# A list schedule with the measured hold of SBUF, K in one piece, and one square sum for V

## The chip, the cores and the metric

The kernel runs on one core of a Trainium2 chip. The core has five instruction queues that matter here: PE (TensorE, matmuls and their weight loads), DVE (VectorE), ACT (ScalarE), POOL (GpSimd) and SP, which here only issues DMAs. Each queue runs its instructions strictly in the order in which they stand; an instruction that waits holds all that stand behind it. The metric is the device time of one execution in microseconds (us); the time before is the median of three runs.

## The reference

```python
def _attn_ref(q, k, v):                         # B=8, H=8, S=1152, D=64
    q_pool = q.reshape(B, H, S // 2, 2, D).mean(axis=3)
    scores = 1 / np.sqrt(D) * np.matmul(q_pool, k.transpose(0, 1, 3, 2))
    attn = softmax(scores)                      # over the keys, row maximum subtracted
    return np.matmul(attn, v)

def _moe_ref(x, w_in, w_spatial, b_spatial, w_out):   # x: 8 x 576 x 512
    h = np.maximum(x @ w_in, 0.0)               # 512 x 1024
    u, v = h[..., :512], h[..., 512:]
    v_n = (v - v.mean(-1)) / np.sqrt(v.var(-1) + 1e-06)
    v_s = np.einsum('ts,bsd->btd', w_spatial, v_n) + b_spatial[None, :, None]
    return (u * v_s) @ w_out
```

All inputs are fp32 (two weight matrices are fp64 in DRAM). The kernel keeps nearly fp32 accuracy with fp16 matmuls: each factor is scaled by a power of two and split into a head (its fp16 value) and a rest (what the head leaves), and the products head x head, head x rest and rest x head are summed.

## The kernel before, in words

**Attention.** The 64 heads are taken as 32 pairs, `i = 0 .. 31`. For a pair, `prep(i)` makes the split factors: squares of K and of the pooled Q are summed on ACT (L569, L571, through `square_sum`, L381), a small matmul with ones (L360) and a few DVE operations (L365 to L371) turn the sums into scales, ACT writes the heads (`head`, L384), and the rests are written by DVE (`rest`, L387: `src * scale - head`, two inputs in SBUF) in the first eight pairs (`i < EARLY`), and by POOL in the others (L605, after ACT has scaled K in place, L602, and copied it to fp16, L604). K is worked on in two pieces of 640 and 512 columns. DMAs on SP (L591 to L614) then copy heads and rests to the partitions where the matmuls want them. `maxima(i)` runs 27 matmuls of 128x384 (L641, and L632 for the middle tile) and after each a DVE reduction (L647); `shift` (L660 to L670) makes of the row maxima a small tile that is transposed on PE (L668) and copied back. Two PSUM buffers (`pm`) serve the maxima, so PE waits for DVE when the reductions fall two behind. `attention(i)` runs the score matmuls (L842, L843) into three PSUM buffers (`pss`), ACT takes exp (L848), POOL splits the fp32 result into a bf16 top and an fp16 rest (L868; two inputs in SBUF), and `values` runs three groups of four small matmuls (L745, L751, L756), the last of which needs POOL's result.

**V.** `norm_v(i)` sums the squares of V, one head at a time (L519), `split_v(i)` writes its head and rest (L543 to L550).

**The gated unit.** After every eight pairs a `gated_unit` of two batches is interleaved with the following pairs: matmuls L926, L990, L1031 and L1074, and on DVE the `normalise` steps (L962 to L974) and at its gate the rests of the gated product (`rest`, L387, tile `vv`). All of these DVE steps read SBUF with two inputs, or in a copying form. There are four units; units 0 to 2 run beside attention, the last alone. In the first eight pairs the weights are loaded and converted from fp64 beside attention, by DVE steps of 128x1024 (L399 to L411).

**What sets the order.** The code is recorded in a rough order, and then `Order.pin` (L187) reorders it: it is a list scheduler that plays the program on the five queues with a cost for each instruction (`cost`, L148) and pins the order that results. Once pinned, nothing of the plan's times is left, only the order on each queue. Of an instruction on lane `m` that needs the result of lane `e`, the planner thinks it due at the result's planned end, plus a delay (`DELAY`), plus a reserve (`SLACK`, L38). For the time in which POOL and DVE hold each other off at SBUF it keeps two marks: `held` is the interval of POOL's last operation, `dve` the end of DVE's last operation of that kind. The operations concerned are those for which `two_from_sbuf` (L182) is true (`shared`). A DVE operation that would start after POOL's planned start is put off to 130 ns before POOL's planned end (L227 to L230, L239 to L247).

Of the kernel before, what the change touches and what calls it, by code (L numbers as in the profile page):

```python
# [10 lines left out]
F16 = mybir.dt.float16  # L11
BF16 = mybir.dt.bfloat16
F32 = mybir.dt.float32
# [18 lines left out]
class Order:  # L32

    LANES = ("PE", "Activation", "DVE", "Pool", "SP")
    DELAY = {("PE", "Activation"): 114, ("Activation", "Pool"): 77}
    SLACK = {("Pool", "PE"): 2100, ("Activation", "PE"): 300, ("DVE", "PE"): 300, ("SP", "PE"): 500}  # L38
    SIZE = {F16: 2, BF16: 2, F32: 4, I32: 4, U32: 4, I64: 8}

    def __init__(self):
# [106 lines left out]
    def cost(self, lane, ins):  # L148

        xs = [x.bass_ap for x in list(ins.ins) + list(ins.outs) if hasattr(x, "bass_ap")]  # L150
        count = lambda ap: math.prod([d[1] for d in ap.ap][1:])
        if lane == "PE":
            n = count(xs[0])
            t = max(28.5, n / 2.4 + 2.5)
            if xs[0].dtype == F32:
                t = 110 if n == 128 else max(224, 4 * n / 2.4)
            return t, t + 148
        if lane == "SP":
            big = max((count(x) * x.ap[0][1] * self.SIZE[x.dtype] for x in xs), default=0)
            return (1230 if "Transpose" in ins.opcode else 560), 2400 + big / (100 if "Transpose" in ins.opcode else 230)  # L160
        n = max((count(x) for x in xs), default=1)
        psum = any(self.slot.get(x.tensor.name, (0, 0))[1] for x in xs)

        flat = sum(count(x) == 1 for x in xs[:-1]) if n > 1 else 0
        wide = len(xs) - 1 - flat
        if lane == "Activation":
            t = 0.84 * n + (157 if psum else 188) + 85 * (min(flat, 2) or (n == 1 and wide > 1))
            if len(ins.outs) > 1:
                return t - 10, t + 95
            return t - 105, t  # L170
        elif lane == "DVE":
            plain = ins.opcode == "TensorScalarPtr"
            if plain and wide < 2 and not psum or ins.opcode == "TensorCopy":
                t = 0.55 * n + 140 + 60 * flat
            else:
                t = 1.04 * n + 145 + 65 * (flat > 0 and plain)
        else:
            t = {F32: 2.1, F16: 2.0, BF16: 1.74}[xs[1].dtype] * n + 150
            return t - 42, t
        return t - 84, t  # L180

# [5 lines left out]
    def pin(self, tc):  # L187
        names = {getattr(mybir.EngineType, e): e for e in self.LANES}
        fixed = ("RegisterMove", "TensorScalarAffineSelect", "Memset")
        prog = [i for i in tc.nc.cur_bb.bb.instructions if i.engine in names and i.opcode not in fixed]  # L190
        before, begun = self.edges(prog)
        loose = {i.name for a, z, skip in self.lined if skip for i in tc.nc.cur_bb.bb.instructions[a:z]}
        early = {i.name for i in tc.nc.cur_bb.bb.instructions[: self.seen]} - loose
        ahead = None
        for n, i in enumerate(prog):
            if names[i.engine] == "SP" and i.name not in loose:
                if ahead is not None and ahead not in before[n]:
                    begun[n].add(ahead)
                if i.name in early:
                    ahead = n  # L200
        after = [[] for _ in prog]
        left = []
        lane = [names[i.engine] for i in prog]
        for n, (pre, beg) in enumerate(zip(before, begun)):
            left.append(len(pre) + len(beg))
            for m in pre:
                after[m].append((n, True))
            for m in beg:
                after[m].append((n, False))
        cost = [self.cost(e, i) for e, i in zip(lane, prog)]  # L210
        shared = [e in ("DVE", "Pool") and self.two_from_sbuf(i) for e, i in zip(lane, prog)]
        held, dve = (0.0, 0.0), 0.0
        ready = {e: [n for n in range(len(prog)) if lane[n] == e and not left[n]] for e in self.LANES}
        due = [0.0] * len(prog)
        there = [0.0] * len(prog)
        free = dict.fromkeys(self.LANES, 0.0)
        wire = 0.0
        load = {n for n, i in enumerate(prog) if lane[n] == "SP" and i.ins and i.ins[0].bass_ap.tensor.name not in self.slot}
        last = {}
        dep = mybir.DependencyInfo(mybir.DependencyClass.NoSync, mybir.DependencyReason.DATA)  # L220
        for _ in prog:
            best = None
            for e, ns in ready.items():
                if ns:

                    at = {n: max(due[n], wire - 1000) if n in load else due[n] for n in ns}
                    if e == "DVE":  # L227
                        for n in ns:
                            if shared[n] and max(free[e], at[n]) >= held[0]:
                                at[n] = max(at[n], held[1] - 130)  # L230
                    t = max(free[e], min(at.values()))
                    n = min(n for n in ns if at[n] <= t)
                    if best is None or t < best[0]:
                        best = (t, e, n)
            t, e, n = best
            ready[e].remove(n)
            own, out = cost[n]
            t = max(free[e], there[n])
            if shared[n]:  # L239

                if e == "DVE":
                    if t >= held[0]:
                        t = max(t, held[1] - 130)
                    dve = t + out
                else:
                    t = max(t, dve)
                    held = (t, t + out)  # L247
            if e == "SP":
                wire = max(wire, t + own) + (out - 2400)
                end = wire + 1700  # L250
            else:
                end = t + out
            free[e] = t + own
            if e in last:
                tc.add_manual_dep(prog[n], last[e], dep, reason="order")
            last[e] = prog[n].name
            for m, through in after[n]:
                left[m] -= 1
                if not through:
                    x = t  # L260
                elif lane[m] != e:
                    x = end + self.DELAY.get((e, lane[m]), 52)
                else:
                    x = t if e == "PE" else end + 34
                there[m] = max(there[m], x)
                due[m] = max(due[m], x + (self.SLACK.get((e, lane[m]), 0) if through else 0))
                if not left[m]:
                    ready[lane[m]].append(m)
        self.span = max(free.values())
# [3 lines left out]
def attn_sgu_kernel(ctx: ExitStack, tc: tile.TileContext, qT, kT, v, w_in, w_spT, b_sp, w_out, out):  # L273
    nc = tc.nc
    P = 128
    B, NHP, _, D, _, S = qT.shape
    NC = kT.shape[4]
# [29 lines left out]
    sm = order.pool(ctx.enter_context(tc.tile_pool(name="sm", bufs=1)), 1)  # L307
# [43 lines left out]
    ws_l = const.tile([P, 5, S], F16, name="ws_l")  # L351
# [28 lines left out]
    def square_sum(acc, src, junk):  # L380
        nc.scalar.activation(junk, src, AF.Square, bias=0.0, scale=1.0, accum_out=acc)  # L381
# [127 lines left out]
    def norm_v(i):  # L509

        b, hp = divmod(i, NHP)
        if hp == 0:
            vsq[b] = sm.tile([P, 2 * NHP], F32, name="vsq", bufs=2)
        vt = load_v(i)
        yield
        yield
        for h in range(2):
            junk = vt[:, h] if b else ws_l[:, 0].rearrange("p (c d) -> p c d", d=D)
            square_sum(vsq[b][:, 2 * hp + h : 2 * hp + h + 1], vt[:, h], junk)  # L519
            yield  # L520
        if hp == NHP - 1:
            vscale[b] = yield from scale_of(vsq.pop(b), "v")
            yield
# [35 lines left out]
    def prep(i):  # L559
# [33 lines left out]
        for h, (a, rows) in enumerate(((MAIN, lower), (0, upper))):  # L593
            nc.sync.dma_start(out=qd[i % 2][rows, h], in_=X[rows, 0, a : a + TAIL])
        kn = st["kn"] = ld.tile([P, NC, P], F16, name="kn")
        for a, z in ((0, 5), (5, NC)):
            if i < EARLY:
                head(kn[:, a:z], k0[:, a:z], s_k)
                yield
                rest(KL[:, 0, a:z], k0[:, a:z], s_k, kn[:, a:z])  # L600
            else:
                nc.scalar.activation(k0[:, a:z], k0[:, a:z], AF.Copy, bias=0.0, scale=s_k)  # L602
                yield
                nc.scalar.activation(kn[:, a:z], k0[:, a:z], AF.Copy, bias=0.0, scale=1.0)  # L604
                nc.gpsimd.tensor_sub(KL[:, 0, a:z], k0[:, a:z], kn[:, a:z])  # L605
            yield
# [627 lines left out]
```

## Time and profile before

| | |
|---|---|
| median of three runs | 1219.08 us (1217.67 to 1220.74) |
| the profiled execution: its own time | 1220.91 us |
| the profiled execution: span of its instructions | 1219.1 us |
| PE busy | 1160.2 us, 95% |
| DVE busy | 887.9 us, 73% |
| ACT busy | 890.8 us, 73% |
| POOL busy | 841.1 us, 69% |
| DMA | 132.97 MB, mean 109 GB/s |

Busy is time in which an engine has an instruction under way. Matmuls overlap in PE's pipeline, and an operation that stands still because another engine holds what it needs counts as busy too; so "busy" is not "at its peak". In the rows, L12 is line 12 of the kernel, `mt<-pm` reads "writes tile mt, reads tile pm", and what stands in square brackets in a timeline is the idle time ahead of an instruction and who ended it.

### The profile page before, as it was taken

The page shows a single profiled execution, that of the slowest core. Times are in us where ns is not written, and L with a number is a line of the kernel's source. Part 1 is how long each engine was busy: PE and PEld are TensorE (multiplying, and loading weights), DVE is VectorE, ACT ScalarE, POOL GpSimd, SP SyncE. Part 2 cuts the span into 40 slices and gives each one's busy share as a digit, 9 for nine tenths or more (in the row PEclk, how much of TensorE's full clock was granted, in tenths as well). Part 3 has the DMA queues.
Part 4 walks back from the last instruction along what each step waited for, and adds up shares of the span by engine and source line. Part 5 has one row for each costly group of instructions (what it writes and reads, how often), then busy time and mean ns, then how long its engine had stood idle before and what let it go on. Part 6 is the DMA issues. An engine that isn't in the chain of part 4 may idle for free.

```text
span 1219.1 us, 33464 instructions
## 1 busy us (share of the span) xinstructions
PE 1160.2 (95%) x13296; PEld 726.5 (60%) x13296; DVE 887.9 (73%) x2228; ACT 890.8 (73%) x1675; POOL 841.1 (69%) x726
## 2 busy tenths in 40 slices
PE   3988999999998999999999999999999999999998
PEld 1656666766655666566665666566665666655453
DVE  5699989987889577766679676865669866841644
ACT  4887779789976877978777877878776876744433
POOL 2545657678886878888887887788887786874000
PEclk9889999999999999999999999999999999999999
DMA  5455455445432454255442443256334421211002
GB/s 190 163 156 161 123 178 143 125 119 153 130 87 77 138 123 123 73 158 152 114 101 75 125 140 82 65 143 204 99 98 103 103 70 49 48 47 45 1 1 79
DMA packets 88446, 132.97 MB, mean 109 GB/s; under 512 B 39840, under 2 KB 48032, under 8 KB 87776
## 3 DMA queue, kind: packets, MB, share of 16 engines
q1 hardware_dynamic: 88288, 130.82, 38.4%
q8 instruction: 104, 1.70, 0.6%
q14 instruction: 54, 0.44, 0.1%
HBM read 81.20 MB, written 9.44 MB: 74 GB/s over the span
## 4 chain that ended last, share of the span: by engine, by line
PE 71%; DVE 22%; issue 2%; ACT 1%; DMA 1%; POOL 0%; SPq 0%; DVEq 0%; ACTq 0%
DVE mt L647 8%; PE pss L842 7%; PE pss L843 7%; PE pm L641 7%; PE pw L1031 7%; PE pw L926 6%; PE pw L1074 5%; PE pw L990 5%; PE o L745 4%; PE o L756 4%; PE o L751 4%; DVE vv L387 2%; PE o L738 1%; DVE row L962 1%; PE pss L926 1%
## 5 line engine op out<-in xcount | busy, mean ns | idle before, releaser
L868 POOL TENSOR_TENSOR pt<-pt 128x512 f16<-128x512 f32 x528 | 574.1, 1103 | 195.8 <-ACT pt L848 193.0
L848 ACT ACTIVATE pt<-pss,esc 128x512 f32<-128x512 f32 x576 | 388.3, 689 | 140.4 <-PE pss L843 124.7
L647 DVE TENSOR_REDUCE mt<-pm 128x1 f32<-128x384 f32 x733 | 387.9, 551 | 102.3 <-PE pm L641 84.0
L842 PE MATMUL pss<-qhi,khi 128*128 128x512 f16 x576 | 220.9, 384 | 2.0 <-ACT pt L848 1.7
L843 PE MATMUL pss<-xq,klo 66*128 66x512 f16 x576 | 221.6, 386 | 0.0
L641 PE MATMUL pm<-khi,qhi 128*128 128x384 f16 x655 | 204.0, 329 | 17.7 <-DVE mt L647 12.6
L745 PEld LDWEIGHTS <-pt 128*128 128x128 bf16 x2112 | 119.3, 99 | 62.2 <-DVE xm L764 6.5
L745 PE MATMUL o<-vp,pt 128*128 128x65 f16 x2112 | 155.1, 193 | 0.7 <-DVE xm L764 0.4
L756 PE MATMUL o<-vp,pt 128*128 128x65 f16 x2112 | 154.1, 193 | 0.0
L751 PE MATMUL o<-vp,pt 128*128 128x64 f16 x2112 | 151.7, 193 | 0.0
L756 PEld LDWEIGHTS <-pt 128*128 128x128 f16 x2112 | 117.7, 98 | 49.5 <-issue 2.7
L641 PEld LDWEIGHTS <-qhi 128*128 128x128 f16 x768 | 74.1, 100 | 70.7 <-issue 28.2
L751 PEld LDWEIGHTS <-pt 128*128 128x128 bf16 x2112 | 101.1, 98 | 3.2 <-issue 0.7
L868 POOL TENSOR_TENSOR ptl<-ptl 128x1152 f16<-128x1152 f32 x32 | 71.7, 2241 | 26.4 <-ACT ptl L864 26.3
L926 PE MATMUL pw<-wi_h,xg 128*128 128x512 f16 x240 | 89.1, 379 | 0.0
L647 DVE TENSOR_REDUCE mt<-pw 128x1 f32<-128x384 f32 x131 | 69.8, 546 | 16.2 <-PE pw L641 16.0
L864 ACT ACTIVATE ptl<-pss,esc 128x256 f32<-128x256 f32 (+1 forms) x128 | 64.0, 500 | 23.5 <-PE pss L859 22.6
L990 PE MATMUL pw<-xg,wi_h 128*128 128x512 f16 (+1 forms) x336 | 80.7, 325 | 0.0
L1074 PE MATMUL pw<-wo_h,vv 128*128 128x512 f16 x216 | 80.1, 379 | 0.6 <-DVE vv L387 0.4
L1031 PE MATMUL pw<-ws_h,vv 128*128 128x512 f16 x216 | 80.2, 379 | 0.0
L843 PEld LDWEIGHTS <-klo 66*128 66x128 f16 x576 | 56.6, 98 | 35.7 <-issue 10.4
L842 PEld LDWEIGHTS <-khi 128*128 128x128 f16 x576 | 56.7, 98 | 27.0 <-issue 6.0
(204 smaller groups left out, 2520.7 us busy)
## 6 DMA issues: line engine op xcount, KB each, us to landing
vt<-in_v_dram SPq DMA_DIRECT2D x56, 576.0 KB
qt<-in_qT_dram SPq DMA_DIRECT2D x32, 576.0 KB
kt<-in_kT_dram SPq DMA_DIRECT2D x32, 576.0 KB
khi<-kn SPq DMA_DIRECT2D x128, 144.0 KB
out_dram<-row SPq DMA_DIRECT2D x24, 256.0 KB
qhi<-xq SPq DMA_DIRECT2D x64, 72.0 KB
klo<-klo SPq DMA_DIRECT2D x32, 144.0 KB
vv<-in_w_in_dram SPq DMA_DIRECT2D x4, 1024.0 KB
```

Source lines behind the costliest of these rows:

```text
L641: nc.tensor.matmul(pm[:, :W], lhsT=qhl[:, h, c0 : c0 + P], rhs=khh[:, h, n * NB : (n + 1) * NB, :], start=True, stop=True,)
L647: nc.vector.reduce_max(out=mt[:, t, n : n + 1], in_=pm[:, :W], axis=AX.X)
L745: nc.tensor.matmul(o[:, t], lhsT=top[:, cols], rhs=vp[:, D : D + D1], start=c == 0 and t == 0, stop=False, skip_group_check=True,)
L751: nc.tensor.matmul(o[:, t, 0:D], lhsT=top[:, cols], rhs=vp[:, 0:D], start=False, stop=False, skip_group_check=True)
L756: nc.tensor.matmul(o[:, t], lhsT=rst[:, cols], rhs=vp[:, D : D + D1], start=False, stop=c == NC - 1, skip_group_check=True,)
L842: nc.tensor.matmul(o, lhsT=khh[:, h, c, :], rhs=qhl[:, h, q], start=True, stop=False)
L843: nc.tensor.matmul(o, lhsT=KL[0:KR, h, c, :], rhs=X[0:KR, h, q], start=False, stop=True)
L848: nc.scalar.activation(pt, ps, AF.Exp, bias=0.0, scale=esc)
L868: nc.gpsimd.tensor_sub(t.bitcast(F16)[..., 0::2], t, t.bitcast(BF16)[..., 1::2])
L926: nc.tensor.matmul(ph, lhsT=xa[:, cc, c0 : c0 + P], rhs=wa[:, cc, DH:DF], start=n == 0, stop=n == 3 * NCC - 1,)
L990: nc.tensor.matmul(pu[:, : z - a], lhsT=wa[:, cc, fc * P : (fc + 1) * P], rhs=xa[:, cc, a:z], start=n == 0, stop=n == 3 * NCC - 1,)
L1031: nc.tensor.matmul(pv, lhsT=l, rhs=r[:, 0:MAIN], **fl)
```

## The change

Four things are changed.

- The planner's account of SBUF. A DVE operation now counts as held off when it would start within `GRAB` = 85 ns of POOL's planned start or later; it is put off to 175 ns (was 130) before POOL's planned end; in the choice among the lanes it is ranked 85 ns later than it is; POOL may start 139 ns before the end of DVE's operation; and every POOL instruction sets the mark.
- The planner's numbers: reserves for PE (POOL 2100 to 1400 ns, DVE 300 to 400, SP 500 to 1000), the cost of an ACT operation that reads PSUM (157 to 162 ns beside its length), and of POOL's operations by type.
- From the third pair on, K's head and rest are made in one piece of 1152 columns instead of 640 and 512: one DVE rest in pairs 2 to 7, and in pairs 8 to 31 one L602, one L604 and one POOL subtraction where there were two of each.
- The squares of V are summed by one ACT operation of 1152 columns for both heads instead of two of 576, with one column for each pair in `vsq`.

```diff
+    GRAB = 85
+    SLACK = {("Pool", "PE"): 1400, ("Activation", "PE"): 300, ("DVE", "PE"): 400, ("SP", "PE"): 1000}
     DELAY = {("PE", "Activation"): 114, ("Activation", "Pool"): 77}
-    SLACK = {("Pool", "PE"): 2100, ("Activation", "PE"): 300, ("DVE", "PE"): 300, ("SP", "PE"): 500}
...
-            t = 0.84 * n + (157 if psum else 188) + 85 * (min(flat, 2) or (n == 1 and wide > 1))
+            t = 0.84 * n + (162 if psum else 188) + 85 * (min(flat, 2) or (n == 1 and wide > 1))
...
-            t = {F32: 2.1, F16: 2.0, BF16: 1.74}[xs[1].dtype] * n + 150
+            t = {F32: 2.17 * n + 150, F16: 1.91 * n + 175, BF16: 1.67 * n + 185}[xs[1].dtype]
...
-                            if shared[n] and max(free[e], at[n]) >= held[0]:
-                                at[n] = max(at[n], held[1] - 130)
+                            if shared[n] and max(free[e], at[n]) + self.GRAB >= held[0]:
+                                at[n] = max(at[n], held[1] - 175)
                     t = max(free[e], min(at.values()))
                     n = min(n for n in ns if at[n] <= t)
-                    if best is None or t < best[0]:
-                        best = (t, e, n)
-            t, e, n = best
+                    key = t + self.GRAB * (e == "DVE" and shared[n])
+                    if best is None or key < best[0]:
+                        best = (key, e, n, t)
+            _, e, n, t = best
...
-            if shared[n]:
-                if e == "DVE":
-                    if t >= held[0]:
-                        t = max(t, held[1] - 130)
-                    dve = t + out
-                else:
-                    t = max(t, dve)
-                    held = (t, t + out)
+            if e == "Pool":
+                t = max(t, dve)
+                held = (t, t + out)
+            elif shared[n]:
+                if t + self.GRAB >= held[0]:
+                    t = max(t, held[1] - 175)
+                dve = t + out - 139
...
-            vsq[b] = sm.tile([P, 2 * NHP], F32, name="vsq", bufs=2)
+            vsq[b] = sm.tile([P, NHP], F32, name="vsq", bufs=2)
...
-        for h in range(2):
-            junk = vt[:, h] if b else ws_l[:, 0].rearrange("p (c d) -> p c d", d=D)
-            square_sum(vsq[b][:, 2 * hp + h : 2 * hp + h + 1], vt[:, h], junk)
-            yield
+        junk = vt if b else ws_l[:, 0:2].rearrange("p h (c d) -> p h c d", d=D)
+        square_sum(vsq[b][:, hp : hp + 1], vt, junk)
+        yield
...
-        for a, z in ((0, 5), (5, NC)):
+        for a, z in ((0, 5), (5, NC)) if i < 2 else ((0, NC),):
```

What this does to the order is seen at three places. In the changed kernel the lines from about L510 on are one lower (L647 is L646 there).

DVE in the fifth pair, about 155 us into the run before, where the second half of the row maxima is turned (`shift`: maximum, scaling, cast and difference, tiles `pw` and `mc`) beside K's rest (`klo`), V's rest (`vp`) and two steps of the weights' conversion (`vv`, `u`). Before:

```order
L387 SCALAR_TENSOR_TENSOR klo_109<-kt,qks,kn 128x512
L409 SCALAR_TENSOR_TENSOR vv<-vv 128x1024
L660 TENSOR_REDUCE pw<-mt 128x4
L387 SCALAR_TENSOR_TENSOR vp_101<-vt,vs,vp_101 128x9x64
L661 TENSOR_SCALAR pw<-pw,lnp 128x4
L647 TENSOR_REDUCE mt<-pw 128x1
L663 CAST mc<-pw 128x4
L647 TENSOR_REDUCE mt<-pm 128x1
L664 TENSOR_TENSOR mc<-pw,mc 128x4
L411 TENSOR_TENSOR u<-u,vv 128x1024
L670 COPY mr<-pw 8x128
```

The same place in the changed kernel:

```order
L659 TENSOR_REDUCE pw<-mt 128x4
L660 TENSOR_SCALAR pw<-pw,lnp 128x4
L662 CAST mc<-pw 128x4
L663 TENSOR_TENSOR mc<-pw,mc 128x4
L409 SCALAR_TENSOR_TENSOR vv<-vv 128x1024
L669 COPY mr<-pw 8x128
L387 SCALAR_TENSOR_TENSOR vp_101<-vt,vs,vp_101 128x9x64
L646 TENSOR_REDUCE mt<-pm 128x1
L646 TENSOR_REDUCE mt<-pw 128x1
L411 TENSOR_TENSOR u<-u,vv 128x1024
```

The four steps of `shift` now stand together ahead of the long steps that read SBUF, and between those stand reductions.

DVE at the gate of unit 1, about 771 us into the run before: the eight rests of the gated product (`vv<-u,gs,vv`) among the reductions of the maxima (`mt<-pm`). Before:

```order
L647 TENSOR_REDUCE mt<-pm 128x1 x2
L387 SCALAR_TENSOR_TENSOR vv<-u,gs,vv 128x576 x2
L647 TENSOR_REDUCE mt<-pm 128x1
L387 SCALAR_TENSOR_TENSOR vv<-u,gs,vv 128x576 x2
L717 TENSOR_SCALAR den<-o 128x4
L647 TENSOR_REDUCE mt<-pm 128x1
L387 SCALAR_TENSOR_TENSOR vv<-u,gs,vv 128x576
L718 RECIPROCAL den<-den 128x4
```

In the changed kernel:

```order
L646 TENSOR_REDUCE mt<-pm 128x1 x5
L387 SCALAR_TENSOR_TENSOR vv<-u,gs,vv 128x576
L646 TENSOR_REDUCE mt<-pm 128x1 x2
L716 TENSOR_SCALAR den<-o 128x4
L717 RECIPROCAL den<-den 128x4
L763 TENSOR_TENSOR xm<-o,den 128x4x64
L387 SCALAR_TENSOR_TENSOR vv<-u,gs,vv 128x576 x2
L646 TENSOR_REDUCE mt<-pm 128x1 x4
L387 SCALAR_TENSOR_TENSOR vv<-u,gs,vv 128x576
```

The first four rests stood two and two, with three reductions ahead of the fourth; now eleven reductions stand ahead of the fourth.

ACT at the start of the program: the squares of K and Q (`klo,sq`), the first square of V (`ws_l,vsq`), and the heads of pair 0 (`xq`, `kn`); - is before, + is the changed kernel.

```order
 L381 ACTIVATE klo_107,sq<-qt 128x576
-L381 ACTIVATE ws_l,vsq<-xg 128x576
-L575 ACTIVATE esc<-qkr 128x1
-L579 ACTIVATE lnp<-qks 128x1
+L381 ACTIVATE ws_l,vsq<-xg 128x1152
+L574 ACTIVATE esc<-qkr 128x1
+L578 ACTIVATE lnp<-qks 128x1
 L384 ACTIVATE xq_113<-qt,qks 128x576
 L384 ACTIVATE kn<-kt,qks 128x640
 L384 ACTIVATE kn<-kt,qks 128x512
```

The first square of V still stands ahead of pair 0's scales and heads, and it is twice as long.

## The prediction

> **What bounds the kernel now.** First the page, for PE's share of the span.
>
> ```profile
> span 1219.1 us, 33464 instructions
> PE 1160.2 (95%) x13296; PEld 726.5 (60%) x13296; DVE 887.9 (73%) x2228; ACT 890.8 (73%) x1675; POOL 841.1 (69%) x726
> ```
>
> PE is idle for 1219.1 - 1160.2 = 58.9 us. The change takes no matmul away, so it can only gain from these 58.9 us (and from what little the pipeline loses in refilling behind each stop). Next the busy time by stretches, cut where PE stops. Columns: window, its length, busy us of PE, PEld, DVE, ACT and POOL (instructions in brackets), granted clock, DMA share, GB/s.
>
> ```profile
> 0.00:60.00 60.00, 38.90 (x312) 22.74 (x313) 35.79 (x93) 37.71 (x77) 24.39 (x30) 0.86 0.54 179
> 60.00:300.00 240.00, 220.02 (x2571) 155.05 (x2571) 222.97 (x511) 197.82 (x371) 156.03 (x121) 0.97 0.49 144
> 350.00:382.00 32.00, 27.53 (x321) 16.80 (x319) 31.04 (x64) 20.26 (x40) 24.26 (x19) 1.00 0.38 99
> 645.00:675.00 30.00, 27.27 (x327) 16.66 (x326) 28.71 (x58) 19.43 (x37) 20.69 (x18) 1.00 0.28 74
> 770.00:782.00 12.00, 10.44 (x136) 6.11 (x135) 11.05 (x20) 9.62 (x18) 7.83 (x7) 1.00 0.01 2
> 927.00:957.00 30.00, 27.41 (x333) 16.82 (x330) 28.71 (x58) 18.85 (x37) 20.96 (x19) 1.00 0.29 77
> 1060.00:1070.00 10.00, 8.29 (x117) 5.37 (x115) 9.97 (x14) 6.80 (x13) 9.80 (x8) 1.00 0.22 55
> 1070.00:1219.00 149.00, 145.24 (x1187) 77.23 (x1185) 62.67 (x159) 61.94 (x110) 33.97 (x33) 1.00 0.11 35
> ```
>
> PE's idle time lies in four places. The start (0 to 60 us) has 60 - 38.90 = 21.1 us, the conversion stage (60 to 300) 20.0, the end (from 1070) 3.8. In between only the five short stretches count: 4.47 + 2.73 + 1.56 + 2.59 + 1.71 = 13.1 us; they are the normalising and the gates of the gated units. That makes 58.0 of 58.9; the rest of the program has PE busy without a break, so DVE, ACT and POOL cost nothing there. In the conversion stage DVE is busy 222.97 of 240 us, in the five stretches 109.5 of 114. So where PE stops, DVE is the bound. PE's own list of waits names it:
>
> ```profile
> PE pm L641 <- DVE mt L647: 12.6, 24, 1.2
> PE pw L641 <- DMA khi<-kn: 7.6, 1, 7.6
> PE pw L668 <- DVE mc L664: 7.5, 7, 2.1
> ```
>
> The columns are total us, times, longest. PE waits for reductions (L647) and for the small tile of `shift` (L664). What keeps DVE from these is seen in the timeline at the place whose order is shown above, engines DVE, POOL and PE:
>
> ```profile
> 155.37 2.06 DVE L409 SCALAR_TENSOR_TENSOR vv<-vv 128x1024 int32<-128x1024 int32 x1
> 156.61 2.08 POOL L566 TENSOR_TENSOR qt<-qt 128x576 f32<-128x576 f32 x1 [0.26 <-DMA qt<-in_qT_dram]
> 157.43 1.88 DVE L387 SCALAR_TENSOR_TENSOR vp<-vt,vs,vp 128x576 f16<-128x576 f32 x1
> 160.35 0.15 DVE L664 TENSOR_TENSOR mc<-pw,mc 128x4 f16<-128x4 f32 x1
> 160.55 0.22 PE L668 MATMUL pw<-ident_h,mc 128*8 128x128 f16 x1 [2.12 <-DVE mc L664]
> ```
>
> The V rest takes 1.88 us and ends about when POOL's operation ends; `shift` stands behind it, and PE stops for 2.12 us. At the gate of unit 1:
>
> ```profile
> 764.13 1.40 POOL L566 TENSOR_TENSOR qt<-qt 128x576 f32<-128x576 f32 x1 [1.81 <-DMA qt<-in_qT_dram]
> ...
> 766.68 10.08 POOL L868 TENSOR_TENSOR pt<-pt 128x512 f16<-128x512 f32 x9
> ...
> 772.77 3.08 DVE L387 SCALAR_TENSOR_TENSOR vv<-u,gs,vv 128x576 f16<-128x576 f32 x2
> ```
>
> Two rests take 3.08 us beside POOL's row of nine. How much of such a duration is hold is told by the last unit, beside which POOL no longer runs: first the same forms from 1140 us on, then those of 300 to 1100 us (mean ns of one behind the busy us).
>
> ```profile
> L387 DVE SCALAR_TENSOR_TENSOR xg<-u,gs,xg 128x576 f16<-128x576 f32 x8 | 6.2, 814 | 3.7 <-ACT xg L384 3.7
> ```
>
> ```profile
> L962 DVE TENSOR_SCALAR row<-vv,mv,rs 128x512 f32<-128x512 f32 x9 | 4.6, 543 | 0.2
> ```
>
> ```profile
> L387 DVE SCALAR_TENSOR_TENSOR vv<-u,gs,vv 128x576 f16<-128x576 f32 x24 | 26.5, 1137 | 0.0
> ```
>
> ```profile
> L962 DVE TENSOR_SCALAR row<-vv,mv,rs 128x512 f32<-128x512 f32 x27 | 23.4, 876 | 0.1
> ```
>
> The hold is 24 x (1137 - 814) = 7.8 us on the gate's rests and 27 x (876 - 543) = 9.0 us on L962. In the conversion stage (mean in the window 60 to 300, then the shortest, middle and longest of L402):
>
> ```profile
> L411 DVE TENSOR_TENSOR u<-u,vv 128x1024 f32<-128x1024 f32 x6 | 11.4, 1906 | 0.0
> L402 DVE SCALAR_TENSOR_TENSOR u<-vv,u 128x1024 f32<-128x1024 uint32 x6 | 11.3, 1884 | 0.0
> ```
>
> ```profile
> L402 DVE SCALAR_TENSOR_TENSOR u<-vv,u x6: 1214/1658/3133, 64.9 to 243.9; 128x1024 f32<-128x1024 uint32 x6
> ```
>
> Taking L402's shortest, 1214, for both, 6 x (1906 - 1214) + 6 x (1884 - 1214) = 8.2 us are hold on two lines alone.
>
> The Trainium skill (SBUF — State Buffer, Who interferes with whom) says that a Vector instruction with two inputs in SBUF and a GpSimd instruction that reads SBUF exclude each other for the whole of the one that came first; the 543 and 876 ns agree. By that rule a better order does not make a hold shorter unless the DVE operation starts in a gap of POOL's.
>
> **The change part by part.**
>
> *Instructions saved.*
>
> ```profile
> L381 ACT ACTIVATE vt<-vt 128x576 f32<-128x576 f32 x56 | 38.5, 691 | 3.4 <-DMA vt<-in_v_dram 3.4
> L381 ACT ACTIVATE klo<-kt 128x1152 f16<-128x1152 f32 x32 | 37.1, 1159 | 4.8 <-DMA kt<-in_kT_dram 4.8
> ...
> L602 ACT ACTIVATE kt<-kt,qks 128x640 f32<-128x640 f32 x24 | 20.0, 832 | 0.0
> ...
> L602 ACT ACTIVATE kt<-kt,qks 128x512 f32<-128x512 f32 x24 | 17.5, 727 | 0.0
> ```
>
> A V square of 1152 should take what K's takes, 1159: it saves 2 x 691 - 1159 = 223 ns, 32 times 7 us, and 32 reads of the accumulator. L602 in one piece is 727 + 640 x (832 - 727) / 128 = 1252 by the two rows' slope, which saves 307 ns in each of 24 pairs; that is 7 us, and L604 should save about as much. So ACT sheds some 21 us and the reads, and PE does not finish sooner for it: in the five stretches ACT is busy 74.96 of 114 us, and outside them PE does not stop. Were ACT the bound, the cover gone, it would be worth up to those. I take 0.
>
> ```profile
> L605 POOL TENSOR_TENSOR klo<-kt,kn 128x640 f16<-128x640 f32 x24 | 34.2, 1427 | 0.0
> ```
>
> ```profile
> L605 POOL TENSOR_TENSOR klo<-kt,kn 128x512 f16<-128x512 f32 x24 | 28.7, 1194 | 2.4 <-ACT kn L604 2.2
> ```
>
> POOL in one piece: 1194 + 640 x (1427 - 1194) / 128 = 2359 instead of 2621 ns, 6.3 us less in 24 pairs. It is hidden the same way: 0. The piece is also a longer hold (a rival below). The six DVE rests of pairs 2 to 7 in one piece save at least the fixed part of an instruction and perhaps one hold: 0.1 to 0.4 us each on a stage that DVE bounds, and they hold back the reductions behind them for longer; I take 1 us in all, within the conversion stage's term. The DMAs of K's heads wait for the whole of K before and after, so SP's copies start no later for it; a piece that ends later would be covered by the two pairs' lead that `prep` has.
>
> *The start.* The first V square stands ahead of pair 0's scales and heads and is 1159 - 691 = 0.47 us longer. The heads, the copies of K and the 7.6 us for which PE waits for them move by it: +0.5 us. The bounds are 0 (if the scales come later than the square ends) and 0.5.
>
> *The reserves for PE.* PE's list of waits has no row that names POOL, so 2100 ns was enough. With 1400 ns, a split that comes late by more stops PE. POOL was late by 1.81 us at 764 us, where it waited for Q; such a place would stop PE for 1.81 - 1.4 = 0.4 us, and delays of that kind were few. Bounds: 0, and 24 x 0.4 = 10 us if it came in each later pair; I take +1 us, near the lower end since no wait is seen now. The 100 ns more for DVE and 500 ns more for SP only move matmuls back among others that are ready: 0.
>
> *The order on DVE.* At the gates, the rests now stand apart among reductions, so that one hold at a time stands ahead of them; two gates showed 1.56 and 1.71 us idle. `shift` no longer stands behind conversion steps at the place shown. Upper bound: all 13.1 us of the stretches and the hold in the conversion stage. Lower bound: nothing, or less, if the holds only fall elsewhere; DVE is busy 96% in the stretches, so not all of it can go without shorter holds. I take half of the 13.1, 6.5 us, and of the conversion stage 4 us (half of the 8.2 us of hold on its two lines, K's 1 us included).
>
> *Sum.* -6.5 - 4 + 0.5 + 1 = -9 us. The profiled execution took 1220.91 us (span 1219.1, and 1.8 around it), 1.83 above the median; from its time I get 1211.9, for the median 1219.08 - 9 = 1210.1 us. About 0.3% (3.7 us) is what a measurement of this kernel can tell from no change.
>
> **The rivals.**
>
> *No change.* The plan's times part from the real ones by more than 85 or 175 ns wherever a DMA or an earlier hold comes between, so DVE meets POOL as often as before. For it: the present plan already avoids holds, with 130 ns, and means of 1137 and 1906 came of it. Against: runs of two to four such steps are gone from the order, whatever the timing. It gives the 1.5 us of the start and the reserve, less K's 1 and a little: 1218 us.
>
> *Slower, by K's longer piece on POOL.* A DVE operation caught behind it stands up to 2359 ns instead of 1427, and reductions behind it. At 0.4 us in each of 24 pairs (9.6 us) the gain of 9 us is gone, and at 0.8 us, nearly the whole of the longer hold, 24 x 0.8 - 9 = 10 us are lost: 1219.08 + 10 = 1229 us. Against: outside the stretches DVE has slack, and PE would have to use up both `pm` buffers.
>
> *A larger gain.* If the stretches lose nearly all their idle time and the conversion stage the 8.2 us of hold on the two lines and as much on its others (half of that reaching PE), 13 + 10 = 23 us: 1196 us. The clock of 0.97 in the conversion stage (0.03 x 240 = 7 us) could come back with it.
>
> **How the numbers follow.** The forecast has 0.50 (1203 to 1215 us, with a quarter to all of the five stretches and of the two lines' hold gained), no change 0.20 (1215 to 1222), slower 0.17 (1223 to 1231), the larger gain 0.13. Faster by over 0.3% is the forecast, the larger gain and a little of no change: 0.65. Within: 0.18. Slower: 0.17. The range 1197 to 1221 leaves out the slower case and the lowest of the larger gain.
>
> **What would show it.** Right: DVE's L387 `vv` below 1000 ns in the mean, PE idle in the five stretches below 8 us, and in the conversion stage below 17; L668's waits shorter. Wrong: a row of PE that waits for POOL (the reserve), a mean of L647 or L387 `qhi` that stands longer in pairs 8 to 31 beside L605 (the long piece), or the same idle time with means as before (no change).

## The result, and the profile after

| | before | changed |
|---|---|---|
| median, us | 1219.71 (4 runs, 1217.67 to 1220.74) | 1201.18 (4 runs, 1200.2 to 1203.26) |
| ratio | | 0.9852, 95% interval 0.9833 to 0.9871 |
| the profiled execution: own time, span | 1220.91, 1219.1 | 1200.2, 1198.4 |

The change saves 18.5 us, twice the 9 that were forecast. The granted clock of the two profiled executions is the same to 0.1% (0.987 and 0.986). All medians here and below are of fast executions; one execution of E3 took 6643 us in the slow state and is left out. From the page of the changed kernel:

```profile
PE 1155.5 (96%) x13296; PEld 729.1 (61%) x13296; DVE 860.1 (72%) x2222; ACT 877.7 (73%) x1557; POOL 842.7 (70%) x702
```

PE is idle for 1198.4 - 1155.5 = 42.9 us, 16.0 less than before. The rest of the 20.7 us between the two spans, 4.7 us, is in PE's busy time. It fits the refilling of the pipeline, whose size isn't shown: at 51.67 us matmuls of 0.38 us start 0.22 us apart, so behind a stop one of them counts for about 0.16 us more (an estimate from these two numbers). Plans at another granted clock have another busy time (E5 below at 0.981 has 1163.8 us, E7 at 0.991 has 1152.0), but the clock is the same in this pair. DVE is busy for 27.8 us less, and its held lines are shorter, as shown below; the new account alone (E1 below) takes off 22.4 us, with as many DVE instructions as before. The busy time by the same stretches, each cut where it lies now (columns as before: PE, PEld, DVE, ACT, POOL, clock, DMA share, GB/s):

```profile
0.00:60.00 60.00, 37.96 (x273) 22.31 (x274) 33.48 (x82) 34.75 (x63) 24.64 (x30) 0.82 0.54 179
60.00:300.00 240.00, 227.07 (x2720) 163.06 (x2718) 220.48 (x529) 203.13 (x356) 165.61 (x125) 0.97 0.53 155
342.00:374.00 32.00, 31.56 (x375) 19.71 (x373) 28.05 (x68) 24.07 (x45) 26.66 (x22) 1.00 0.37 98
637.00:667.00 30.00, 29.55 (x353) 18.20 (x352) 27.19 (x69) 21.45 (x40) 22.56 (x20) 1.00 0.24 62
755.00:767.00 12.00, 11.86 (x162) 7.49 (x161) 10.88 (x25) 12.00 (x24) 10.85 (x11) 1.00 0.12 23
914.00:944.00 30.00, 29.55 (x356) 18.26 (x355) 27.20 (x68) 21.45 (x39) 22.57 (x19) 1.00 0.26 63
1030.00:1040.00 10.00, 8.94 (x112) 5.04 (x110) 8.79 (x18) 8.53 (x15) 6.17 (x7) 1.00 0.01 2
```

In the five stretches PE stands for 0.44 + 0.45 + 0.14 + 0.45 + 1.06 = 2.5 us, where it stood for 13.1. In the conversion stage it stands for 12.9 instead of 20.0 us. In the first 60 us it stands 0.9 us longer and does 273 matmuls instead of 312, at a granted clock of 0.82 instead of 0.86. PE's own waits (total us, times, longest):

```profile
PE pw L640 <- DVE mt L646: 8.1, 9, 3.2
PE pw L640 <- DMA khi<-kn: 8.0, 1, 8.0
PE pw L667 <- DVE mc L663: 4.0, 5, 1.8
...
PE pm L640 <- DVE mt L646: 1.9, 5, 0.5
```

The wait of the `pm` maxima for DVE, 12.6 us before, is 1.9; that for `shift` 4.0 instead of 7.5; that for K's first heads 8.0 instead of 7.6. One wait grew, that of the `pw` maxima, which lies in the conversion stage for the most part. It was 5.4 us before and is 8.1:

```profile
PE pw L641 <- DVE mt L647: 5.4, 7, 2.0
```

At the gate of unit 1, the timeline of DVE and POOL:

```profile
758.02 0.81 DVE L387 SCALAR_TENSOR_TENSOR vv<-u,gs,vv 128x576 f16<-128x576 f32 x1
...
760.76 1.54 DVE L387 SCALAR_TENSOR_TENSOR vv<-u,gs,vv 128x576 f16<-128x576 f32 x2
...
761.70 1.50 POOL L867 TENSOR_TENSOR pt<-pt 128x512 f16<-128x512 f32 x1 [0.97 <-ACT pt L847]
```

The first three rests run at their unheld length (0.81 us, and two in 1.54), and where one of them and POOL's split meet, it is POOL that takes longer, 1.50 us; the shortest split of this kernel takes 1.03. Before, the first two alone took 3.08. The same two lines of DVE from 300 to 1100 us, then the two conversion steps from 60 to 300 us (mean ns of one behind the busy us):

```profile
L387 DVE SCALAR_TENSOR_TENSOR vv<-u,gs,vv 128x576 f16<-128x576 f32 x24 | 23.7, 999 | 0.0
...
L961 DVE TENSOR_SCALAR row<-vv,mv,rs 128x512 f32<-128x512 f32 x27 | 19.3, 717 | 0.1
```

```profile
L402 DVE SCALAR_TENSOR_TENSOR u<-vv,u 128x1024 f32<-128x1024 uint32 x6 | 9.3, 1552 | 0.0
...
L411 DVE TENSOR_TENSOR u<-u,vv 128x1024 f32<-128x1024 f32 x6 | 7.7, 1276 | 0.0
```

They were 1137, 876, 1884 and 1906 ns.

### The profile page after: what moved, and what is told of

Same layout as the page of the kernel before. It is cut to its first block, busy times and chain, and to the rows that moved or that the text cites. A ratio compares the mean times of both kernels' runs of the same rounds, so it can differ in the third digit from the quotient of the medians.

```text
span 1198.4 us, 33324 instructions
## 1 busy us (share of the span) xinstructions
PE 1155.5 (96%) x13296; PEld 729.1 (61%) x13296; DVE 860.1 (72%) x2222; ACT 877.7 (73%) x1557; POOL 842.7 (70%) x702
## 4 chain that ended last, share of the span: by engine, by line
PE 83%; DVE 10%; ACT 2%; DMA 1%; issue 1%; SPq 0%; POOL 0%; DVEq 0%; ACTq 0%
PE pss L841 9%; PE pss L842 9%; PE pm L640 8%; PE pw L1030 7%; PE pw L925 7%; PE pw L1073 6%; PE pw L989 6%; PE o L744 5%; PE o L755 5%; PE o L750 5%; DVE mt L646 4%; PE o L737 3%; PE pss L925 1%; PE pss L858 1%; PE pss L854 1%; PE pss L1030 1%
## 5 line engine op out<-in xcount | busy, mean ns | idle before, releaser
L867 POOL TENSOR_TENSOR pt<-pt 128x512 f16<-128x512 f32 x528 | 580.9, 1117 | 184.7 <-ACT pt L847 180.7
L646 DVE TENSOR_REDUCE mt<-pm 128x1 f32<-128x384 f32 x733 | 389.1, 551 | 104.7 <-PE pm L640 86.0
L842 PE MATMUL pss<-xq,klo 66*128 66x512 f16 x576 | 221.7, 386 | 0.0
L744 PEld LDWEIGHTS <-pt 128*128 128x128 bf16 x2112 | 124.1, 99 | 70.0 <-DVE xm L763 4.1
L750 PE MATMUL o<-vp,pt 128*128 128x64 f16 x2112 | 154.3, 194 | 0.0
L755 PEld LDWEIGHTS <-pt 128*128 128x128 f16 x2112 | 114.7, 98 | 37.1 <-issue 1.4
L750 PEld LDWEIGHTS <-pt 128*128 128x128 bf16 x2112 | 102.9, 98 | 3.9 <-issue 1.0
L1073 PE MATMUL pw<-wo_h,vv 128*128 128x512 f16 x216 | 78.9, 379 | 1.1 <-DVE vv L387 0.7
L842 PEld LDWEIGHTS <-klo 66*128 66x128 f16 x576 | 56.5, 98 | 32.9 <-issue 8.9
L646 DVE TENSOR_REDUCE mt<-pw 128x1 f32<-128x384 f32 x131 | 70.0, 546 | 6.4 <-PE pw L640 5.9
L549 POOL TENSOR_TENSOR vp<-vt,vp 128x576 f16<-128x576 f32 x48 | 60.5, 1260 | 18.4 <-ACT vp L547 18.0
```

Source lines behind the costliest of these rows:

```text
L646: nc.vector.reduce_max(out=mt[:, t, n : n + 1], in_=pm[:, :W], axis=AX.X)
L744: nc.tensor.matmul(o[:, t], lhsT=top[:, cols], rhs=vp[:, D : D + D1], start=c == 0 and t == 0, stop=False, skip_group_check=True,)
L750: nc.tensor.matmul(o[:, t, 0:D], lhsT=top[:, cols], rhs=vp[:, 0:D], start=False, stop=False, skip_group_check=True)
L755: nc.tensor.matmul(o[:, t], lhsT=rst[:, cols], rhs=vp[:, D : D + D1], start=False, stop=c == NC - 1, skip_group_check=True,)
L842: nc.tensor.matmul(o, lhsT=KL[0:KR, h, c, :], rhs=X[0:KR, h, q], start=False, stop=True)
L867: nc.gpsimd.tensor_sub(t.bitcast(F16)[..., 0::2], t, t.bitcast(BF16)[..., 1::2])
```

## The experiments

The theory (A) was that the planner's new account of SBUF makes the gain, since it changes what stands ahead of what on DVE. The rivals were the fewer and larger instructions (M), the new reserves and costs (N), and chance (C): any other plan lands some us away. Twelve kernels were run; their times stand together here. "Pair 8" is the start of the 145th score matmul L842 (18 for each pair) in the profiled execution, "8 to 31" the time from there to the 559th. Between 31 and the end all took 133.7 to 134.2 us.

| kernel | account | median, us | ratio to before (95%) | pair 8, us | 8 to 31, us |
|---|---|---|---|---|---|
| before | old | 1219.71 | 1 | 276.2 | 809.2 |
| E2 merges alone | old | 1220.44 | 1.0008 (0.9996 to 1.002) | 275.0 | 809.9 |
| E3 reserves and costs alone | old | 1213.8 | 0.9948 (0.9928 to 0.9968) | 274.4 | 806.4 |
| E4 delay 120 | old | 1211.44 | 0.993 (0.9915 to 0.9946) | 268.5 | 806.5 |
| E8 delay 108 | old | 1211.69 | 0.9922 (0.9904 to 0.9941) | 272.9 | 804.2 |
| E5 changed, old account | old | 1213.49 | 0.9938 (0.9917 to 0.9958) | 272.3 | 806.5 |
| E10 as E5, and 85 ns | old | 1217.95 | 0.9984 (0.9973 to 0.9995) | 273.8 | 808.3 |
| E9 changed, no account | none | 1231.12 | 1.0086 (1.0064 to 1.0108) | 270.2 | 820.8 |
| changed | new | 1201.18 | 0.9852 (0.9833 to 0.9871) | 268.0 | 796.4 |
| E1 account alone | new | 1203.9 | 0.987 (0.9853 to 0.9887) | 266.4 | 801.9 |
| E7 changed, old reserves and costs | new | 1205.21 | 0.9874 (0.9853 to 0.9895) | 264.4 | 807.0 |
| E11 changed, old costs | new | 1202.07 | 0.9853 (0.9836 to 0.987) | 265.9 | 798.3 |
| E6 changed, delay 120 | new | 1201.52 | 0.984 (0.9821 to 0.986) | 269.7 | 797.8 |
| E12 changed, first V square halved | new | 1195.86 | 0.9803 (0.979 to 0.9815) | 263.1 | 797.0 |

### One part alone: E1, E2, E3, and a control, E4

E1 puts the account alone into the kernel before: `GRAB` and the two pieces of `pin` as in the diff of the change. E2 puts in K in one piece and the V squares alone, E3 the `SLACK` line and the costs alone. E4 moves a number that has nothing to do with SBUF:

```diff
-    DELAY = {("PE", "Activation"): 114, ("Activation", "Pool"): 77}
+    DELAY = {("PE", "Activation"): 120, ("Activation", "Pool"): 77}
```

Expected of E1:

> The kernel before with the planner's new account of SBUF alone (GRAB, the 175 ns, the ranking, POOL's start 139 ns before DVE's end); reserves, costs, pieces of K and squares of V stay as before. If the account makes the gain (theory A), 1202 to 1209 us, with the mean of L962 and of the gate's rests as low as in the changed kernel (673 and 999 ns). If fewer and larger instructions make it (theory M), or the reserves and costs (theory N), 1216 to 1221 us and means near 793 and 1137 ns.

Of E2:

> The kernel before with K in one piece from the third pair on and one square sum for V, planner untouched. Theory M: 1203 to 1210 us. Theory A: 1216 to 1222 us, since ACT and POOL are hidden and DVE saves 1 to 2 us. If K's longer piece on POOL holds DVE up, over 1222 us.

Of E3:

> The kernel before with the new reserves and costs alone. Theory N: 1203 to 1210 us. Theory A: 1215 to 1223 us; with POOL's shorter reserve a row of PE waiting for POOL may show up, 1 us or less.

Of E4:

> A control: the kernel before with one planner number that has nothing to do with SBUF moved by 6 ns (the delay from PE to ACT, 114 to 120), which makes another plan of the same quality. If plans differ by chance as much as the gain (theory C), it lies more than 5 us from 1219; if not, within 3 us.

E1 took 1203.9 us: the account alone gives 16 of the 18.5 us. E2 gives nothing, though ACT is busy for 11 us less than before (879.4 against 890.8) and DVE for 9 (879.3 against 887.9); so what was said to be hidden is hidden, and theory M falls. E3 gives 6 us and lies in neither range that was expected. The control gives 8.5, much more than the 3 that theory A allowed it. It refuted that part of the theory: chance is of a size with a good part of the gain, and one pair of plans proves little. In E1 the account shows in the DVE lines from 300 to 1100 us:

```profile
L387 DVE SCALAR_TENSOR_TENSOR vv<-u,gs,vv 128x576 f16<-128x576 f32 x24 | 28.1, 1190 | 0.0
...
L962 DVE TENSOR_SCALAR row<-vv,mv,rs 128x512 f32<-128x512 f32 x27 | 19.5, 734 | 0.1
```

L962 is as short as in the changed kernel, but the gate's rests, against the expectation, are no shorter than before (1137).

### More plans of each kind: E5, E6, E7, E8

E5 is the changed kernel with the old account, E7 the changed one with the old `SLACK` and costs. E6 moves `DELAY` from 114 to 120 in the changed kernel, E8 from 114 to 108 in the kernel before.

Expected of E5:

> The changed kernel with the old account of SBUF: new reserves, costs, pieces of K and squares of V are kept. Theory A (the account makes the gain in the gated stretches): pair 8 to pair 31 takes 805 us or more again, as before and unlike the 796 us of the changed kernel, DVE busy above 870 us, and 1208 to 1220 us in all. Theory N or M with the account as a bystander: 1205 us or less.

Of E6:

> A control: the changed kernel with the delay from PE to ACT moved from 114 to 120 ns, as in the control of before. Theory A: within 5 us of 1201, and its time from pair 8 to pair 31 at most 800 us. Theory C (chance): anywhere from 1195 to 1215 us, with no difference between the kind of account.

Of E7:

> The changed kernel with the old reserves and costs: account, pieces of K and squares of V as in the changed one. Theory A: 1200 to 1205 us, as the account alone gave 1203.9. If the reserves and costs add to it, 1206 us or more.

Of E8:

> A second control of the kernel before: the delay from PE to ACT 108 instead of 114 ns. With the first (1211.4 us) it says how wide plans of the old account lie. Theory A: 1208 to 1222 us in all, pair 8 to pair 31 between 803 and 812 us, DVE busy above 870 us. Theory C: it may come to 1203 us or less.

The two kinds don't overlap. The seven plans of the old account have ratios from 0.9922 to 1.0008, with a mean of 0.9961; the six of the new one, E11 and E12 included, 0.9803 to 0.9874, with a mean of 0.9849. The difference, 0.0113 or 13.7 us, is what the account is worth on the average plan; the spread of so few plans leaves some 4 us of doubt either way (an estimate from the thirteen ratios, as if the plans were independent). E10 is counted as old here, though it has one part of the new account. The kernel before was with E2 at the slow end of its kind, 4.7 us above its mean, and the changed kernel at the mean of its own. So theory A holds for about three quarters of the gain, and theory C for the rest.

The same can be done by stages, from the last two columns. At pair 8 the means of the two kinds are 273.3 and 266.3 us, 7 apart, where this pair of kernels has 8.2. From pair 8 to 31 they are 807.3 and 799.7, 7.6 apart, where this pair has 12.8. So most of what does not belong to the account alone lies after pair 8; the reserves have a part in that, as E11 will show. Plans of one kind differ by up to 8 us at pair 8 and, but for E7, by 6 from there to pair 31.

E7 stands out: 807.0 us from pair 8 to 31, no better than the old account, and 0.2 us above the range that theory A gave for the whole. In sum its holds are as short as in the changed kernel: the gate's rests, L961 and L967 are together busy for 64.8 us from 300 to 1100 us, for 63.6 in the changed kernel, and for 73.4 before. But it is the normalise steps that are short in E7, while the gate's rests are long; what PE meets stands at the head of its list of waits from 300 to 1060 us:

```profile
L387 DVE SCALAR_TENSOR_TENSOR vv<-u,gs,vv 128x576 f16<-128x576 f32 x24 | 28.8, 1207 | 0.0
...
L961 DVE TENSOR_SCALAR row<-vv,mv,rs 128x512 f32<-128x512 f32 x27 | 17.2, 636 | 0.1
```

```profile
PE pw L1073 <- DVE vv L387: 3.0, 6, 1.0
```

The matmuls that use the gate's rests (L1073) come too early for some of them, here six times.

### No account, one part of it, and the costs: E9, E10, E11

E9 is the changed kernel with a planner that holds nothing off:

```diff
-        shared = [e in ("DVE", "Pool") and self.two_from_sbuf(i) for e, i in zip(lane, prog)]
+        shared = [False] * len(prog)
...
-            if e == "Pool":
-                t = max(t, dve)
-                held = (t, t + out)
-            elif shared[n]:
+            if shared[n]:
```

E10 is E5 with `+ 85` in the two tests against `held[0]`. E11 is the changed kernel with the old costs of ACT and POOL; its reserves are the new ones.

Expected of E9:

> The changed kernel with a planner that knows nothing of SBUF: no DVE operation is put off and POOL waits for none; the rest as changed. Theory A: the hold on DVE is at least that of the old account and the time 1212 us or more. If the old account was worth nothing, it comes out as the changed kernel with the old account did (1213.5 us); if the new one is worth nothing either, near 1201.

Of E10:

> The changed kernel with the old account, plus one of its parts: a DVE operation counts as held off from 85 ns ahead of POOL's planned start. 130 ns, ranking and POOL's start stay as before. If that part makes the account's gain, 1200 to 1205 us and the hold on DVE after 300 us near 33 us; if the putting off by 175 ns, the ranking and POOL's 139 ns make it, 1209 to 1216 us and a hold near 46 us.

Of E11:

> The changed kernel with the old costs of ACT and POOL and the new reserves. If the reserves shorten the wait of the gate's products for DVE's rests (4.9 us without the new numbers, 1.7 with them), 1200 to 1203 us and pair 8 to pair 31 near 797 us. If the costs do it, 1204 to 1208 us and about 807.

E9 took 1231.12 us, by the ratios 18 us more than E5 with the old account and 29 more than the changed kernel. It is one plan only, but it lies some 10 us beyond the slowest of the old account. The sum of the holds is not what makes E9 slow: against the expectation it is no larger than before. The gate's rests, L958 and L964 are together busy for 73.4 us from 300 to 1100 us, as their like before, and DVE as a whole is less busy; PE all the same is idle for 800 - 780.69 = 19.3 us there, where it was idle for 800 - 786.09 = 13.9. First E9, then the kernel before:

```profile
L384 DVE SCALAR_TENSOR_TENSOR vv<-u,gs,vv 128x576 f16<-128x576 f32 x24 | 27.9, 1180 | 0.0
...
L958 DVE TENSOR_SCALAR row<-vv,mv,rs 128x512 f32<-128x512 f32 x27 | 21.6, 825 | 0.2
```

```profile
300.00:1100.00 800.00, 780.69 (x9471) 484.39 (x9470) 569.75 (x1489) 595.54 (x1051) 637.14 (x535) 1.00 0.37 102
```

```profile
300.00:1100.00 800.00, 786.09 (x9599) 489.70 (x9598) 576.66 (x1499) 609.83 (x1146) 648.36 (x565) 1.00 0.40 105
```

E9's waits of PE from 300 to 1060 us are headed by the small tile of `shift`. Three of the four, 6.6 us in all, are one in each unit, and the first looks like this:

```profile
PE pm L664 <- DVE mc L660: 7.0, 4, 2.2
PE pm L637 <- DVE mt L643: 3.9, 8, 0.9
```

```profile
362.95 2.41 POOL L601 TENSOR_TENSOR klo<-kt,kn 128x1152 f16<-128x1152 f32 x1
...
363.24 2.27 DVE L968 COPY te<-vv 64x512 f16<-64x512 f16 x1
...
365.54 0.17 DVE L660 TENSOR_TENSOR mc<-pm,mc 128x5 f16<-128x5 f32 x1
...
365.76 0.22 PE L664 MATMUL pm<-ident_h,mc 128*10 128x128 f16 x1 [2.21 <-DVE mc L660]
```

POOL's subtraction of K, in one piece, holds a copy on DVE for 2.27 us (the same copy takes 0.29 in E11); the last step of `shift` stands behind it in DVE's queue, and PE waits for that step's tile. So the longer piece on POOL, one of the rivals, does harm where something urgent stands behind it.

E11 says the same from the other side. Its holds on the three lines are as long as those of the old account (76.4 us together), and yet PE is idle for 800 - 794.72 = 5.3 us alone, and the time is that of the changed kernel:

```profile
L387 DVE SCALAR_TENSOR_TENSOR vv<-u,gs,vv 128x576 f16<-128x576 f32 x24 | 29.0, 1217 | 0.0
...
L961 DVE TENSOR_SCALAR row<-vv,mv,rs 128x512 f32<-128x512 f32 x27 | 22.8, 845 | 0.3
```

```profile
300.00:1100.00 800.00, 794.72 (x9720) 496.93 (x9718) 562.33 (x1490) 603.75 (x1070) 652.16 (x546) 1.00 0.37 103
```

So the sum of the holds doesn't give the time; what stands behind a held step does. Against E7, E11 also shows what the new reserves do: 798.3 us from pair 8 to 31 instead of 807.0. The table says it for all plans. The four with the new account and the new reserves (changed, E6, E11, E12) take 796.4 to 798.3 us there, the two with the new account and the old reserves (E1, E7) 801.9 and 807.0, and the seven of the old account 804.2 to 809.9, with the new reserves (E3, E5, E10) or without. In this stage account and reserves make the gain together, and the reserves alone make none that shows. With the old costs and the short reserve PE does stand for POOL, which the changed kernel never shows (E11, same list of waits):

```profile
PE pw L1073 <- DVE vv L387: 2.5, 2, 1.3
PE o L755 <- POOL pt L867: 0.8, 2, 0.7
```

E10 took 1217.95 us, more than either range that was expected, with gate's rests of 1407 ns in the mean. The 85 ns in the tests alone show no gain; it lies in the other parts (175 ns, the ranking, POOL's start 139 ns before DVE's end, the mark that every POOL instruction sets) or in all of them together. Which, was not tried.

### The start: E12

```diff
-        square_sum(vsq[b][:, hp : hp + 1], vt, junk)
-        yield
+        if i == 0:
+            square_sum(vsq[b][:, NHP : NHP + 1], vt[:, 1], junk[:, 1])
+            yield
+            square_sum(vsq[b][:, 0:1], vt[:, 0], junk[:, 0])
+        else:
+            square_sum(vsq[b][:, hp : hp + 1], vt, junk)
+        yield
```

(`vsq` has one column more for the first batch.)

Expected of E12:

> The changed kernel with the first pair's V squares in two halves again, the first of which stands where the one square stood, ahead of the heads. K's heads then reach the matmuls at 16.2 us after the start, as before, and not at 16.6, and the kernel takes about 1200.7 us, 0.5 less than the changed one, which is below what the timing resolves: the trace has to show it.

ACT's first V square in the changed kernel and what follows it, then the square in E12:

```profile
8.49 1.15 ACT L381 ACTIVATE ws_l<-xg 128x1152 f16<-128x1152 f32 x1
9.54 0.19 ACT L381 ACTIVATION_READ_ACCUMULATOR ws_l<-xg 128x1 f32 x1
```

```profile
8.44 0.67 ACT L381 ACTIVATE ws_l<-xg 128x576 f16<-128x576 f32 x1
```

And PE's first maxima matmul, again in this order:

```profile
16.77 0.48 PE L640 MATMUL pw<-khi,qhi 128*128 128x384 f16 x1 [7.98 <-DMA khi<-kn]
```

```profile
16.35 0.48 PE L645 MATMUL pw<-khi,qhi 128*128 128x384 f16 x1 [7.61 <-DMA khi<-kn]
```

The first matmul has its 0.4 us back. E12 took 1195.86 us, by the ratios 6 less than the changed kernel, where 0.5 was expected, so it beats both. Nearly all of that has come by pair 8 (263.1 against 268.0 us), but not from the first matmul: by 30 us both kernels have done 34 matmuls, by 50 us E12 is 15 behind. Then it gets ahead, as the windows of 50 to 80 us show, the changed kernel first:

```profile
50.00:80.00 30.00, 24.25 (x208) 16.75 (x204) 20.78 (x54) 17.20 (x29) 9.25 (x8) 0.72 0.65 220
```

```profile
50.00:80.00 30.00, 24.75 (x280) 17.14 (x280) 26.43 (x63) 21.12 (x36) 13.01 (x10) 0.89 0.65 215
```

PE is busy about as long in both, but at a granted clock of 0.72 and 0.89, and E12 does 72 matmuls more. Of the new kind the two plans at 0.72 there (changed, E6) start pair 8 latest, at 268.0 and 269.7 us; E11, which has the one square too, has 0.89 and 265.9. But the clock is not shown to be the cause: in the old kind no such order shows (before 0.89 and 276.2, E5 0.66 and 272.3), and two executions of the changed kernel have E12's clock over the whole (0.989) and took 1201.0 and 1201.4 us. Plans of one kind differ by as much, so the 6 us may be chance; nothing was run that tells.

## Why the prediction was right, and where it was off

- *What bounds, and where.* Right. PE's idle time went where it was said to be, in the five stretches and the conversion stage, and nothing was gained where PE did not stop: the end takes as long as before.
- *The saved instructions are worth nothing.* Right (E2: 1.0008, 0.9996 to 1.002). The length of one came near: K's L602 in one piece takes 1256 ns (1252 by the slope), POOL's subtraction 2468 (2359). The sum did not: ACT is busy for 13.1 us less, not 21 and the reads. Operations on ACT that follow each other overlap (the V square of 1.15 us starts at 8.49, what follows at 9.54, 0.10 before its end), so lengths added up say too much.
- *The start, +0.5 us.* Right for the first matmul, which comes 0.47 us later (16.30 to 16.77 us), and in part luck: over all traces it comes at 16.43 to 16.77 us with one square and at 16.16 to 16.35 with two, 0.3 apart in the mean. That it costs the whole 0.5 us isn't shown, since by 30 us the kernel before, the changed one and E12 have all done 34 matmuls.
- *The reserve of POOL, +1 us.* Wrong: no row of PE waits for POOL in the changed kernel, so it is 0. E11 shows what the term meant, 0.8 us, when the costs of POOL are the old ones.
- *The order on DVE, stretches, -6.5 us.* The mechanism was right and the size was off: 13.1 to 2.5 us is -10.5, and from pair 8 to 31 it is 809.2 - 796.4 = 12.8 with what PE's busy time lost, at a granted clock of 1.00 in both. By the means of the two kinds it is 7.6, and against the plans with the new reserves 10. The half was taken because "not all of it can go without shorter holds". That step was too low: in E11 the holds on the three lines are as long as before, and PE stands for 5.3 us from 300 to 1100 us instead of 13.9. It is enough that nothing urgent stands behind the hold. One sign of being right, gate's rests below 1000 ns in the mean, was met by 1 ns and says little: E11 has the gain with 1217.
- *The conversion stage, -4 us.* Mis-sized too: pair 8 starts 8.2 us earlier, the 0.5 of the start included. By the means of the two kinds it is 7, so about 1 us is chance; why half of the two lines' hold was too little was not tried.
- *The rivals.* "No change" was argued from plans that part from the real times; they do, since holds remain (999 ns for 814), but the order helps all the same. The longer piece of K on POOL did no harm in the changed kernel: DVE's Q rest, which stands beside it, has a mean of 1055 ns instead of 1031 over all pairs, 32 x 24 ns = 0.8 us in sum, and PE didn't stop for it. In E9 it did harm, as shown above. The forecast left out one thing, that a plan of the same quality can lie 8 us away; it would have widened its range rather than moved it.
- *A line read for another.* The prediction finds the rule on instructions with two inputs borne out by the 543 and 876 ns of L962. That line reads one tile of full width and two single columns; the line with two full inputs is that of the gate's rests, and its 814 and 1137 ns show the hold.

## What to carry to other kernels

Where a DVE operation can be held off by POOL, don't count the held time; look at what stands behind it in DVE's queue and who waits for that. Put steps of the critical kind (here the reductions and `shift`) ahead of or between the ones that can be held, and give the consumers of the spread steps a longer reserve. And before crediting a change in a scheduler's numbers, move a number that should not matter: here that alone moved the time by 8 us, and only several plans of each kind told the gain from chance.

## What was not expected of the hardware

A hold can go either way, and the order on the queues decides which. In the changed kernel POOL's splits got longer (1103 to 1117 ns in the mean of 528, 7 us in sum) while DVE's held lines got shorter, and PE never waited for a split:

```profile
L867 POOL TENSOR_TENSOR pt<-pt 128x512 f16<-128x512 f32 x528 | 580.9, 1117 | 184.7 <-ACT pt L847 180.7 <-DMA qhi<-xq 1.6
```

POOL stands idle for 184.7 us ahead of these splits, so a hold put on POOL cost nothing here, with 1.4 us in the plan for its results; with the same reserve and the old costs (E11) it cost PE 0.8 us. This is the Trainium skill's rule (SBUF — State Buffer, Who interferes with whom), that the one which issues first blocks the other, seen from its useful side; the gate at 760 us shows it with 1.54 us for two unheld rests and 1.50 for the held split.
